# Attention's preparation in a new order: loads ahead of operand copies, norms of six heads on GpSimd, decoding by slot 94

## The chip, the cores and the metric

The program runs on one core of one Trainium2 chip. The metric is device time in microseconds, one launch from start to end. The core's engines are TensorE (PE; its weight loads are listed as PEld), VectorE (DVE), ScalarE (ACT), GpSimd (POOL) and SyncE (SP), which here only issues DMAs. Each engine takes its instructions in the order of the program and stands at one whose semaphores have not come; an instruction that runs on another engine is waited for by semaphore.

## The reference, cut to what matters

```python
# q, k, v: (2, 8, 768, 64); centroids: (8, 16, 64)
q_assign = argmax(einsum('bhsd,hcd->bhsc', q / norm(q), c / norm(c)))     # nearest of 16 centroids
k_assign = argmax(einsum('bhsd,hcd->bhsc', k / norm(k), c / norm(c)))
mask     = q_assign[..., :, None] == k_assign[..., None, :]
scores   = where(mask, q @ k.T / 8, -1e9);  attn = softmax(scores)        # with the maximum taken out
x        = attn @ v                                                       # to (1536, 512)
h = x @ w_in;  x = (max(h, 0) + alpha * min(h, 0)) @ w_out                # 512 -> 2048 -> 512
xn = x / sqrt(mean(x * x) + 1e-6) * rms_g
g = xn @ w_gate;  out = (g * sigmoid(g) * (xn @ w_val)) @ w_out2          # 512 -> 1536 -> 512
```

Everything is float32. The kernel's matmuls run on rounded operands (fp32r) split into a high and a low part.

## The kernel before

Attention takes the 16 heads as 8 pairs. A pair has two phases, one for each half of its queries, and a phase has six slots, one for each tile of 128 keys; so a pair is 12 slots, attention is slots 0 to 95, and slots before 0 prepare. The body of slot s is `st_tile` (L522): for each of the two heads two matmuls make scores (L532, L533) and ScalarE takes the exponential (L534) out of one of three score banks. Every second slot `pv_tiles` multiplies two tiles by the values (L548) and sums them (L553). Nine slots ahead, `max_tile` makes the scores of a later phase once more, without their low parts (L490), into its one bank (two PSUM banks wide), and VectorE takes the maxima (L494); `max_split` and `max_rows` (L499 to L519) put them as two rows into the operand op2. At a phase's end come the sums, their reciprocals and the product (L560 to L598).

A pair is prepared some 40 slots ahead. SP loads the rows ("nat") and their transposes ("raw") of q and k (`load`, L340, L342). ScalarE squares nat (L350); VectorE, or for pair 1 GpSimd in halvings (L361), sums the squares (L364); fourteen small steps on VectorE, on 24 numbers a partition, make the norms (`rnorm`, L321 to L328). ScalarE casts raw to the high part in a stage (L449), GpSimd subtracts for the low part (L454). TensorE makes the similarities with the centroids (L380, L390), VectorE scales them (L397), finds the nearest centroid and writes a one-hot code (L406 to L419), TensorE transposes it (L428). There are two stages, pair by pair in turn, and one nat and one raw tile. SP then copies stage and code into the operands op1 and op2 (`prep_dma_a` L458, `prep_dma_oh` L471, `prep_dma_b` L465 to L467), which have room for two pairs: the copies of pair p stand in slots 12p - 12 to 12p - 10, behind the last score matmul of pair p - 2, and the stage they read is written again by the cast of pair p + 2.

The order of everything is written out by hand. The tables FIRST to PAIR give for each kind of step its slot (relative to the pair's first) and a number that sorts it within the slot; the maxima's slots of phases 0, 2 and 3 stand in AHEAD, the others are LEAD = 9 slots ahead of their use. `plan` puts all of it into slots, and `slot` emits it, so this order is the order of each engine's queue, SP's too:

```python
"load": ((-38, 6.1), (-38, 6.2), (-35, 6.1), (-35, 6.2)),     # PAIR: nat q, nat k, raw q, raw k
"hi": ((-33, 4), (-32, 4)),
at(b - 12, 2.5, self.prep_dma_a, h + e)
at(b - 11 + e, 2.5, self.prep_dma_b, h + e)
```

Behind attention stand two feed-forward layers of TensorE work (`mm3`, L796). Their weights come as 64-bit numbers and are decoded in halves: `decode_step` is one of four steps of a half, two groups on VectorE (L772 to L778), a cast on ScalarE (L785), and the low part on GpSimd or VectorE (L782, L783). The first eight halves, 32 steps, are placed by hand among attention's slots in EARLY and TAIL; TAIL also holds the first up and down projections of the first layer (L842 to L898).

Of the kernel before, what the change touches and what calls it, by code (L numbers as in the profile page):

```python
# [13 lines left out]
ALU = mybir.AluOpType  # L14
# [8 lines left out]
    "load": ((-38, 6.1), (-38, 6.2), (-35, 6.1), (-35, 6.2)),  # L23
# [5 lines left out]
    "sims": ((-30, 1.7), (-29, 1.7)),  # L29
    "scale": ((-29, 5.9),),  # L30
# [9 lines left out]
    "norm": tuple((-27 + n // 5, 5 + (n % 5) / 10) for n in range(14)),  # L40
# [3 lines left out]
    "scale": ((-24, 5.1),),  # L44
    "arg": ((-22, 5), (-21, 5), (-20, 5), (-19, 5), (-17, 5)),
    "oht": ((-13, 1.7),),
}
THIRD = {
    **PAIR,
    "load": ((-27, -0.2), (-27, 6), (-26, 6), (-26, 6.1)),  # L50
    "sq": ((-25, 4), (-24, 4)),
    "ss": ((-24, 5), (-23, 5)),
    "norm": tuple((-23 + n // 5, 5.1 + (n % 5) / 10) for n in range(14)),
# [54 lines left out]
    (-1, 8.5, "decode_step"),
    (-2, 9, "decode_step"),
    (-2, 0.95, "decode_step"),  # L110
    (0, 1.45, "decode_step"),
    (2, 1.5, "decode_step"),
    (1, 10, "decode_step"),
# [18 lines left out]
    (1, 4, "decode_step"),  # L132
    (1, 4.1, "decode_step"),
    (1, 4.2, "decode_step"),
    (1, 4.3, "decode_step"),
    (2, 0.2, "decode_step"),
    (2, 0.3, "decode_step"),
# [38 lines left out]
class Attention:  # L176
# [175 lines left out]
    def prep_ss(self, pr, i):  # L352
# [4 lines left out]
        if pr == 1:  # L357
# [7 lines left out]
        if i == 1:  # L365
            self.norm[pr] = self.rnorm(self.ss.pop(pr), [128, X, 2, 4], f"n{pr % 2}")
# [233 lines left out]
    def plan(self):  # L600
# [3 lines left out]
        def at(s, o, fn, *a):  # L604
            ev.setdefault(s, []).append((o, len(ev.get(s, [])), fn, a))
# [530 lines left out]
```

## Time and profile before

| | |
|---|---|
| median of 3 runs | 943.79 us (941.26 to 945.05) |
| profiled execution | 944.59 us, its span 942.8 us |
| busy of the span | TensorE 878.1, VectorE 609.1, GpSimd 376.9, ScalarE 325.3 us |
| mean granted clock of TensorE | 0.96 |

The profile is one execution, and its times count from the span's start. A row of the timeline gives start and length in us, engine, line, operation, result and operands, and in brackets how long the engine had been idle and what ended that. Matmuls that follow each other overlap. An idle engine costs time only where something that sets the end waits for it.

### The profile page before, as it was taken

The page shows a single profiled execution, that of the slowest core. Times are in us where ns is not written, and L with a number is a line of the kernel's source. Part 1 is how long each engine was busy: PE and PEld are TensorE (multiplying, and loading weights), DVE is VectorE, ACT ScalarE, POOL GpSimd, SP SyncE. Part 2 cuts the span into 40 slices and gives each one's busy share as a digit, 9 for nine tenths or more (in the row PEclk, how much of TensorE's full clock was granted, in tenths as well). Part 3 has the DMA queues.
Part 4 walks back from the last instruction along what each step waited for, and adds up shares of the span by engine and source line. Part 5 has one row for each costly group of instructions (what it writes and reads, how often), then busy time and mean ns, then how long its engine had stood idle before and what let it go on. Part 6 is the DMA issues. An engine that isn't in the chain of part 4 may idle for free.

```text
span 942.8 us, 11565 instructions
## 1 busy us (share of the span) xinstructions
PE 878.1 (93%) x4358; PEld 646.2 (69%) x4358; DVE 609.1 (65%) x928; ACT 325.3 (35%) x623; POOL 376.9 (40%) x301
## 2 busy tenths in 40 slices
PE   6787797887999998999999998999999999999998
PEld 4444454555565656877888777787788888888886
DVE  7865663635546646587877988778995838484222
ACT  4344343345444542334343334443322212221111
POOL 5301102011000035466666767523684637464111
PEclk8599797989999999999999999999999999999999
DMA  6946152707147011121221322100231212120002
GB/s 187 227 125 153 54 121 73 162 32 181 41 108 191 25 61 52 39 73 68 68 67 48 109 79 78 45 1 23 90 104 52 90 45 90 44 68 1 1 24 110
DMA packets 24279, 75.69 MB, mean 80 GB/s; under 512 B 3680, under 2 KB 4896, under 8 KB 24224
## 3 DMA queue, kind: packets, MB, share of 16 engines
q1 hardware_dynamic: 24224, 74.96, 27.7%
q8 instruction: 34, 0.56, 0.2%
q14 instruction: 21, 0.17, 0.1%
HBM read 51.46 MB, written 3.15 MB: 58 GB/s over the span
## 4 chain that ended last, share of the span: by engine, by line
PE 70%; DVE 16%; issue 5%; ACT 4%; DMA 3%; POOL 2%; SPq 0%; ACTq 0%; POOLq 0%; DVEq 0%
PE ps_st L796 23%; PE ps_mx L796 10%; PE ps_pv L796 9%; PE ps_pv L548 7%; PE ps_pr L796 4%; PE ps_mx L490 4%; PE ps_pv L553 4%; PE ps_st L532 3%; DVE dec_a L774 3%; PE ps_st L533 3%; DVE x L898 2%; DVE dec_a L772 2%; DMA nat<-in_qn_dram 1%; DVE mx L494 1%; PE ps_pr L581 1%
## 5 line engine op out<-in xcount | busy, mean ns | idle before, releaser
L494 DVE TENSOR_REDUCE mx<-ps_mx 128x1 f32<-128x768 f32 x93 | 88.9, 956 | 113.0 <-PE ps_mx L490 113.0
L856 POOL TENSOR_TENSOR gl<-v,gh 128x512 fp32r<-128x512 f32 x68 | 94.7, 1393 | 101.0 <-ACT gh L855 101.0
L534 ACT ACTIVATE p<-ps_st 128x384 f32<-128x384 f32 x192 | 83.8, 494 | 63.9 <-PE ps_st L533 62.9
L532 PE MATMUL ps_st<-op 128*128 128x384 f32 x192 | 73.7, 384 | 18.5 <-ACT p L534 18.5
L598 POOL TENSOR_TENSOR x1l<-X,x1h 128x384 fp32r<-128x384 f32 x15 | 15.2, 1015 | 184.0 <-ACT x1h L595 184.0
L796 PE MATMUL ps_st<-x1h,stage 128*128 128x512 f32 x272 | 84.3, 391 | 0.0
L774 DVE SCALAR_TENSOR_TENSOR dec_a<-raw,dec_a 128x512 uint32<-128x512 uint32 x66 | 82.4, 1248 | 2.3
L855 ACT CAST gh<-v 128x512 fp32r<-128x512 f32 x68 | 42.2, 621 | 114.5 <-DVE v L852 64.1
L548 PE MATMUL ps_pv<-p,vnat 128*64 128x384 f32 x384 | 78.1, 531 | 0.0
L852 DVE TENSOR_TENSOR v<-ps_st,t 128x512 f32<-128x512 f32 x36 | 24.8, 690 | 77.1 <-PE ps_st L796 76.9
L848 DVE SCALAR_TENSOR_TENSOR v<-v,alpha,t 128x512 f32<-128x512 f32 x45 | 44.9, 999 | 43.4 <-ACT v L847 43.4
L533 PE MATMUL ps_st<-op 82*128 82x384 f32 x192 | 68.0, 354 | 0.0
L454 POOL TENSOR_TENSOR stage<-raw,stage 128x768 fp32r<-128x768 f32 x16 | 29.0, 1825 | 93.4 <-ACT stage L449 77.8
L490 PE MATMUL ps_mx<-op 80*128 80x384 f32 x186 | 56.4, 386 | 8.8 <-DVE mx L494 8.8
L782 POOL TENSOR_TENSOR dec_a<-dec_a,woh 128x512 f32<-128x512 f32 x27 | 42.9, 1590 | 43.1 <-ACT woh L785 39.6
L490 PEld LDWEIGHTS ps_mx<-op 80*128 80x128 f32 x186 | 33.1, 203 | 38.3 <-issue 18.5
L796 PEld LDWEIGHTS ps_st<-x1h,stage 128*128 128x128 f32 x272 | 50.9, 188 | 10.9
L796 PE MATMUL ps_st<-x1h,wvh 128*128 128x512 f32 x144 | 57.0, 396 | 0.9 <-ACT t L851 0.9
L898 DVE TENSOR_TENSOR x<-ps_mx,x 128x1024 f32<-128x1024 f32 x36 | 43.8, 1218 | 21.6 <-PE ps_mx L796 21.6
L532 PEld LDWEIGHTS ps_st<-op 128*128 128x128 f32 x192 | 38.3, 199 | 27.7 <-ACT p L534 25.4
L796 PE MATMUL ps_st<-x1h,wvl 128*128 128x512 f32 x144 | 56.9, 395 | 0.0
L796 PE MATMUL ps_st<-x1l,wvh 128*128 128x512 f32 x144 | 56.8, 394 | 0.0
(247 smaller groups left out, 2105.1 us busy)
## 6 DMA issues: line engine op xcount, KB each, us to landing
raw<-in_moe_w_out_dram SPq DMA_DIRECT2D x28, 512.0 KB, 3.6
op<-stage SPq DMA_DIRECT2D x32, 384.0 KB, 5.5
raw<-in_moe_w_in_dram SPq DMA_DIRECT2D x15, 512.0 KB, 3.6
raw<-in_moe_w_val_dram SPq DMA_DIRECT2D x12, 512.0 KB, 3.4
raw<-in_moe_w_gate_dram SPq DMA_DIRECT2D x12, 512.0 KB, 3.4
op<-stage SPq DMA_DIRECT2D x16, 288.0 KB, 6.5
nat<-in_qn_dram SPq DMA_DIRECT2D x8, 384.0 KB, 4.3
nat<-in_kn_dram SPq DMA_DIRECT2D x8, 384.0 KB, 5.3
```

The lines of the kernel that those rows point to most:

```text
L490: nc.tensor.matmul(ps[:, g, :self.HS], lhsT=o1[0:80, 0, t * 128:(t + 1) * 128], rhs=o1[0:80, 1, sl], start=True, stop=True)
L494: nc.vector.tensor_reduce(out=self.mx[ph][:, k:k + 1], in_=ps[:, :, :self.HS], op=ALU.max, axis=AX.XY)
L532: nc.tensor.matmul(ps, lhsT=o1[:, 1, ks], rhs=o1[:, 0, qs], start=True, stop=False)
L533: nc.tensor.matmul(ps, lhsT=o2[:, 1, ks], rhs=o2[:, 0, qs], start=False, stop=True)
L534: nc.scalar.activation(out=p[:, e], in_=ps, func=AF.Exp, scale=self.scale)
L548: nc.tensor.matmul(ps[64 * e:64 * e + 64], lhsT=self.vnat[ph // 2][:, e, t0 + y], rhs=P[y][:, e], start=t0 + y == 0, stop=t0 + y == T - 1)
L774: v.scalar_tensor_tensor(out=a, in0=top, scalar=0xC0000000, in1=a, op0=ALU.bitwise_and, op1=ALU.bitwise_or)
L782: eng.tensor_tensor(out=af, in0=af, in1=f(hi), op=ALU.subtract)
L796: self.nc.tensor.matmul(ps, lhsT=a, rhs=b, start=first and i == 0, stop=last and i == len(terms) - 1)
L848: nc.vector.scalar_tensor_tensor(out=v, in0=v, scalar=self.nalpha[:, a], in1=t, op0=ALU.mult, op1=ALU.add)
L856: nc.gpsimd.tensor_tensor(out=lo, in0=v, in1=f(hi), op=ALU.subtract)
L898: nc.vector.tensor_tensor(out=dst, in0=ps, in1=dst, op=ALU.add)
```

## The change

It moves steps between slots and engines; what is computed stays.

- Loads: nat and raw of pairs 5 to 7 go from slots -38 and -35 (relative to the pair) to -41, -39 and -38; pair 4 gets a table of its own, FIFTH, with its raw loads first in slot 13 and its casts three slots later; pair 2's nat loads go from slot -3 to -6, pair 3's stay.
- Norms: for pairs 1, 2 and 3 (six heads) the sums of squares are halvings on GpSimd, and of each Newton round four steps run on GpSimd instead of three on VectorE. The first two and the last three steps stay on VectorE. Pair 1's are put ahead of its second low part.
- Maxima: phase 1's six go from slots -3 to 2 to slots -1 to 4; those of phases 2 and 3 begin one slot later.
- Order within a slot: the scaling right behind the similarities' transposes, the sums' matmul behind the maximum and the score matmuls instead of ahead of them, the similarities behind the product with the values.
- Decoding: all 24 steps of TAIL by slot 94 (-2 from attention's end); ten of them stood in slots 95 to 98. For it the second weight buffer of the down projection is opened with the first pool instead of at attention's end.

```diff
 PAIR = {
-    "load": ((-38, 6.1), (-38, 6.2), (-35, 6.1), (-35, 6.2)),
+    "load": ((-41, 6.1), (-41, 6.2), (-39, 6.1), (-38, 6.1)),
-    "sims": ((-30, 1.7), (-29, 1.7)),
-    "scale": ((-29, 5.9),),
+    "sims": ((-30, 2.5), (-29, 1.7)),
+    "scale": ((-29, 1.75),),
 FOURTH = {
-    "norm": tuple((-27 + n // 5, 5 + (n % 5) / 10) for n in range(14)),
+    "norm": tuple((-27 + n // 6, 5 + (n % 6) / 10) for n in range(17)),
-    "scale": ((-24, 5.1),),
+    "scale": ((-24, 1.75),),
+FIFTH = {
+    **PAIR,
+    "load": ((-37, 6.1), (-37, 6.2), (-35, 1.8), (-35, 1.9)),
+    "hi": ((-30, 4), (-29, 4)),
+    "lo": ((-29, 4.5), (-28, 4.5)),
+}
 THIRD = {
-    "load": ((-27, -0.2), (-27, 6), (-26, 6), (-26, 6.1)),
+    "load": ((-30, 13), (-30, 13.1), (-26, 6), (-26, 6.1)),
-    "norm": tuple((-23 + n // 5, 5.1 + (n % 5) / 10) for n in range(14)),
+    "norm": tuple((-23 + n // 5, 5.1 + (n % 5) / 10) for n in range(17)),
 SECOND = {
-    "norm": tuple((-17 + n // 5, 0.3 + (n % 5) / 100) for n in range(14)),
-    "scale": ((-14, 5),),
-    "arg": ((-13, 5.1), (-12, 5), (-11, 5.1), (-10, 5), (-9, 5.1)),
-    "oht": ((-8, 0.7),),
+    "norm": tuple((-18, 9 + n / 100) for n in range(14)) + tuple((-12, 5 + n / 100) for n in range(3)),
+    "scale": ((-12, 5.1),),
+    "arg": ((-11, 5.1), (-10, 5), (-10, 5.1), (-9, 5), (-9, 5.1)),
+    "oht": ((-8, 2.6),),
 AHEAD = {
     0: (-12, -11, -10, -9, -8, -7),
-    2: (6, 6, 7, 8, 9, 10),
-    3: (10, 11, 12, 13, 14, 15),
+    1: (-1, 0, 1, 2, 3, 4),
+    2: (7, 7, 8, 9, 9, 10),
+    3: (11, 12, 12, 13, 14, 15),
 }
+ASIDE = (1, 2, 3)
 TAIL = (
     (-15, 1.45, "decode_step"),
+    (-14, 9, "decode_step"),
+    (-13, 0.5, "decode_step"),
...
+    (-2, 0.5, "decode_step"),
     (-2, 9, "decode_step"),
-    (-1, 8.5, "decode_step"),
...
-    (1, 4, "decode_step"),
...
-    (2, 0.3, "decode_step"),
+    def rnorm(self, ss, shape, tag, aside=False):
+        g = self.nc.gpsimd
         def newton():
+            if aside:
+                return [
+                    lambda: g.tensor_tensor(out=a, in0=y, in1=ss, op=ALU.mult),
+                    lambda: g.tensor_tensor(out=a, in0=a, in1=y, op=ALU.mult),
+                    lambda: g.tensor_scalar(out=a, in0=a, scalar1=-0.5, scalar2=1.5, op0=ALU.mult, op1=ALU.add),
+                    lambda: g.tensor_tensor(out=y, in0=y, in1=a, op=ALU.mult),
+                ]
     def prep_ss(self, pr, i):
-        if pr == 1:
+        if pr in ASIDE:
-            self.norm[pr] = self.rnorm(self.ss.pop(pr), [128, X, 2, 4], f"n{pr % 2}")
+            self.norm[pr] = self.rnorm(self.ss.pop(pr), [128, X, 2, 4], f"n{pr % 2}", pr in ASIDE)
     def plan(self):
-            tab = (FIRST, SECOND, THIRD, FOURTH, PAIR)[min(pr, 4)]
+            tab = (FIRST, SECOND, THIRD, FOURTH, FIFTH, PAIR)[min(pr, 5)]
-            at(b + (7 if last else 8), -0.5 if last else 0.6, self.out_sums, ph)
-            at(b + (7 if last else 8), -0.4 if last else 0.65, self.out_recip, ph)
+            at(b + (7 if last else 8), -0.5 if last else 1.7, self.out_sums, ph)
+            at(b + (7 if last else 8), -0.4 if last else 1.75, self.out_recip, ph)
     def open(self, early):
-        self.wbuf["wo"] = [self.wpair(one, "wo", 0)]
+        self.wbuf["wo"] = [self.wpair(one, "wo", i) for i in range(2)]
     def more(self, ctx):
-        self.wbuf["wo"].append(self.wpair(one, "wo", 1))
```

## Rows read from the trace of the kernel before

**Rows 1.** Stretches: length, busy us of PE, PEld, DVE, ACT, POOL; clock, DMA share.

```profile
26.40:46.80 20.40, 15.44 (x51) 10.54 (x53) 17.50 (x36) 8.94 (x16) 5.82 (x4) 0.50 0.95 234
...
46.90:81.27 34.37, 27.74 (x180) 14.72 (x176) 21.38 (x59) 13.47 (x29) 3.15 (x2) 0.95 0.35 103
81.27:127.40 46.13, 38.31 (x237) 22.62 (x233) 25.40 (x53) 18.87 (x40) 7.39 (x5) 0.89 0.38 94
127.40:170.37 42.97, 36.54 (x227) 21.39 (x226) 20.76 (x48) 18.46 (x42) 5.84 (x5) 0.88 0.43 106
170.37:212.28 41.91, 35.79 (x225) 21.31 (x225) 21.00 (x48) 18.28 (x41) 5.62 (x4) 0.92 0.45 109
212.28:253.61 41.33, 35.40 (x225) 21.15 (x225) 20.98 (x48) 18.28 (x41) 5.62 (x4) 0.92 0.44 103
253.61:285.82 32.21, 31.31 (x214) 19.35 (x214) 16.46 (x31) 14.89 (x36) 2.01 (x2) 1.00 0.47 109
...
366.00:380.00 14.00, 9.95 (x37) 7.72 (x36) 7.80 (x8) 1.91 (x4) 4.54 (x3) 0.88 0.11 39
```

**Rows 2.** Waits of PE, slots 24 to 59: total us, times, longest.

```profile
PE ps_st L532 <- ACT p L534: 16.3, 9, 4.8
```

**Rows 3.** Timeline of slots 27 to 29.

```profile
146.66 0.83 ACT L449 CAST stage<-raw 128x768 fp32r<-128x768 f32 x1 [7.94 <-DMA vnat<-in_vn_dram]
...
147.93 0.69 PE L532 MATMUL ps_st<-op 128*128 128x384 f32 x1 [4.80 <-ACT p L534]
```

**Rows 4.** Timeline of SP, slots 26 to 28: DMA issues.

```profile
133.39 1.25 SPq L467 DMA_DIRECT2D op<-stage  x1
...
136.76 0.76 SPq L342 DMA_DIRECT2D raw<-in_kt_dram  x1
...
138.78 0.99 SPq L467 DMA_DIRECT2D op<-stage  x1
```

**Rows 5.** DMA issues at 133.39, 136.76, 138.78, 28.21: KB, us to landing.

```profile
op<-stage SPq DMA_DIRECT2D x1, 96.0 KB, 5.3
...
raw<-in_kt_dram SPq DMA_DIRECT2D x1, 384.0 KB, 6.1
...
op<-stage SPq DMA_DIRECT2D x1, 96.0 KB, 7.6
...
op<-stage SPq DMA_DIRECT2D x1, 96.0 KB, 5.2
```

**Rows 6.** Timeline of PE, slots 4 to 6.

```profile
53.16 0.85 PE L380 MATMUL ps_pr<-raw,cb 128*32 128x384 f32 x8
...
56.98 0.49 PE L390 MATMUL ps_pr<-idf,simc 128*128 128x128 f32 x3
...
59.58 0.62 PE L490 MATMUL ps_mx<-op 80*128 80x384 f32 x2 [1.05 <-DVE mx L494]
```

**Rows 7.** Timeline of GpSimd and VectorE, slot 2.

```profile
44.65 3.60 POOL L454 TENSOR_TENSOR stage<-raw,stage 128x768 fp32r<-128x768 f32 x2 [11.25 <-ACT stage L449]
...
44.83 1.69 DVE L315 TENSOR_TENSOR n_a<-n_y,ss 128x24 f32<-128x24 f32 x1
```

**Rows 8.** Instructions of line 315: ns, least, median, most.

```profile
L315 DVE TENSOR_TENSOR n_a<-n_y,ss x24: 173/182/1696, 8.1 to 229.4; 128x24 f32<-128x24 f32 x24
```

**Rows 9.** Timeline of slots -9 to 0.

```profile
28.21 1.53 SPq L467 DMA_DIRECT2D op<-stage  x1
...
34.85 1.01 PE L490 MATMUL ps_mx<-op 80*128 80x384 f32 x2 [2.51 <-DVE mx L494]
...
37.71 0.53 PE L532 MATMUL ps_st<-op 128*128 128x384 f32 x1
```

**Rows 10.** Groups of GpSimd by form: count, busy us, mean ns, idle before.

```profile
L361 POOL TENSOR_TENSOR nat<-nat 128x24 f32<-128x24 f32 x2 | 0.5, 252 | 0.2
```

**Rows 11.** Waits of PE, slots 12 to 23.

```profile
PE ps_pr L581 <- ACT op L519: 2.4, 1, 2.4
```

**Rows 12.** Timeline of PE, the second down projection.

```profile
370.40 0.47 PE L796 MATMUL ps_mx<-gh,woh 128*128 128x512 f32 x1 [4.05 <-DVE x L896]
```

More of the change, by code (lines that the diff above doesn't have):

```diff
@@ L96 @@
     (-15, 1.45, "decode_step"),
+    (-14, 9, "decode_step"),
+    (-13, 0.5, "decode_step"),
+    (-13, 9, "decode_step"),
     (-12, 9, "decode_step"),
-    (-11, 0.5, "decode_step"),
+    (-11, 9, "decode_step"),
+    (-10, 0.5, "decode_step"),
     (-10, 9, "decode_step"),
-    (-8, -0.5, "decode_step"),
-    (-10, 8.95, "decode_step"),
-    (-7, 9, "decode_step"),
-    (-4, 9.0, "decode_step"),
-    (-5, 9, "decode_step"),
+    (-9, 9, "decode_step"),
+    (-9, 9.1, "decode_step"),
+    (-8, 0.5, "decode_step"),
+    (-8, 9, "decode_step"),
+    (-8, 9.1, "decode_step"),
+    (-7, 9, "decode_step"),
+    (-6, 0.5, "decode_step"),
+    (-6, 9, "decode_step"),
+    (-6, 9.1, "decode_step"),
+    (-5, 7, "decode_step"),
+    (-4, 0.5, "decode_step"),
     (-4, 9, "decode_step"),
+    (-4, 9.1, "decode_step"),
     (-3, 9, "decode_step"),
+    (-2, 0.5, "decode_step"),
     (-2, 9, "decode_step"),
-    (-1, 8.5, "decode_step"),
[L109 to L113, printed above, removed]
     (-9, 2.55, "up_part", 0, 0),
@@ L131 @@
     (2, 5, "down_add", 0, 0, 1),
-    (1, 4, "decode_step"),
[L133 to L136, printed above, removed]
-    (2, 0.3, "decode_step"),
     (3, 1, "down_mm", 1, 0, 0),
@@ L305, in warm @@
             self.nc.tensor.matmul(ps, lhsT=self.idr, rhs=self.zero, start=True, stop=True)
-    def rnorm(self, ss, shape, tag):
+    def rnorm(self, ss, shape, tag, aside=False):
         v = self.nc.vector
```

## The prediction

> **What bounds the kernel now.** I read the stages first, in the table of stretches, which I cut where the score matmuls (L532, two in a slot) of slots 0, 12, 24 and so on begin [rows 1]. Slots 60 to 71 compute a pair of heads with nothing of a later pair prepared beside it: 32.21 us, TensorE busy 31.31, granted clock 1.00 (2.4 GHz). The five pairs before it compute the same and take 46.13, 42.97, 41.91, 41.33, and, in slots 0 to 11 (37.7 to 81.27), 43.57. That is 216 us against five times 32.2, 161. The two feed-forward layers behind attention keep their code. So attention's first 60 slots and its last few are what can move.
>
> Then the waits, to see what ends TensorE's idle time there. In slots 24 to 59 nearly all of it is a score matmul that waits for the exponential of an earlier tile [rows 2]: the score banks are full because ScalarE is late. The timeline says why: in slot 27 ScalarE stands for 7.94 us in front of the cast at L449, until 146.66, and TensorE loses 4.80 [rows 3]. The same wait is there one and two pairs later.
>
> What does the cast wait for? It reads a raw tile and writes a stage. The second raw load was issued at 136.76 and took 6.1, so it was there at 142.9, before the cast. But the stage still had readers, the operand copies of two pairs ago: the last was issued at 138.78, took 7.6, and landed at 146.4 [rows 4, 5]. That is the moment at which the cast goes on. So it waits for the copies, and the raw loads matter because they stand in front of those copies: the group of copies ahead of them landed at 133.39 + 5.3 = 138.7, they at 142.9. They hold the queue for 4.2 us.
>
> **The three pairs of slots 24 to 59.** For pairs 5, 6 and 7 the change puts the raw loads (and the nat loads) ahead of that group of copies, into slots 19 to 22, 31 to 34 and 43 to 46, where the last reader of their tile, in slot 20, 30 or 42, has run. The casts stay in slots 27 and 28, the copies in 24 to 26. The copies then land up to 4.2 us earlier, and TensorE's 4.80 becomes 0.6; the other bound is half of the 4.2 (if the copies' own many small pieces set the pace), which leaves 2.7. I take 0.6, as both groups follow the other traffic directly. A pair then costs 32.21, plus the matmuls that prepare a later pair: 0.85 and 0.49 for the similarities [rows 6], some 0.4 for three lighter transposes, 1.75 together. The low clock behind each long wait (stretch clocks 0.88, 0.92, 0.92) goes with the wait. That is 33.96 + 0.6.
>
> A new cost: the low parts (L454) on GpSimd now run in slot 28, where VectorE has its norm steps; till now most of those came before them. How that looks is seen at 44.65: two subtractions on GpSimd take 3.60, and beside them a VectorE step on 24 elements takes 1.69 [rows 7], where the middle one of its kind takes 0.18 [rows 8]. The maximum behind such steps comes late, and TensorE needs its bank. Bounds: 0, and 3.4 for two such steps; I take 1.0, since VectorE is busy for only 21 us of such a pair and catches up. Pair: 35.6; three: 106.8 instead of 126.2. Gain 19.4, bounds 24.3 (neither wait) and 3 (2.7 of wait, 3.4 of VectorE, and 1.0 to 1.7 of low clock in each).
>
> **Start, up to slot 12.** TensorE now reaches slot 0 behind three maxima of phase 1, and these come behind fourteen norm steps on VectorE: the second maximum waits 2.51 for VectorE, and slot 0 begins at 37.71 [rows 9]. The change leaves one maximum in front of slot 0 and puts twelve norm steps of pair 1 on GpSimd. Slot 0 can then begin when the last copies for head 1 are there, 28.21 + 5.2 = 33.4 [rows 9, 5]: four us earlier. It doesn't run fast at once: from 26.4 to 46.8 the granted clock is 0.50 (1.2 GHz) with TensorE busy 76%, and the DMA engines are at 95% [rows 1]. ScalarE's squares and casts of pair 2 stand between the first exponentials and wait for loads on those engines, so I let slot 3 begin near 43.5 instead of 50. Slots 3 to 11 run 1 us shorter: VectorE is freed there of 24 norm steps at 0.18 to 1.7 each and of four sums of squares, but TensorE waits 1.05 in each slot with two maxima, as at 59.58, because they share one bank [rows 6]; two such slots stand there now (6, 10) and two then (7, 9). Gain 7.5, bounds 4 and 10.
>
> GpSimd's price: the trace has no norm step on it. The nearest row is the addition with 24 results, 0.252 us [rows 10]; twelve with small gaps are 3.6 a pair. The squares of pairs 2 and 3 that go with them are six halvings for q and for k, from 384 wide down to 12; between 0.252 for 24 and 1.8 for 768 wide they make about 3 each, an estimate from these rows. That is 10 us a pair on an engine that is busy for 7.39 of the 46 us of slots 12 to 23 [rows 1]. Bounds for a step: 0.2 and 1.8.
>
> The Trainium skill (GPSIMD Engine Reference, 4.1 Engine selection) speaks against this move: elementwise work on two inputs belongs on VectorE, GpSimd being about twice as slow. The rows give 0.252 against 0.18, so 1.4 times at this width. By the page's ratio twelve steps would be about 4.9 with the gaps, and the sum 1.3 higher if pair 1's norms set the start; by the rows they end before the loads for which ScalarE waits.
>
> **Middle, slots 12 to 23.** The casts of pair 4 go from slots 15 and 16 to 18 and 19, when the copies out of their stage have long landed. So the 2.4 that TensorE stood in slot 16 behind ScalarE [rows 11] is gone, and the low clock behind it. The sums' matmul goes behind the maximum, and the scaling goes first on VectorE, so that one waits less for the other. At clock 1.00 the work of a pair is 31.3, plus 2.2 of preparation (three of its four parts and one twice), plus one more maximum and one more row of maxima, 1.3: 34.8. I leave 4.1 idle: 2.1 in two slots with double maxima, the usual 0.9 (32.21 - 31.31), 1.1 of small waits. 38.9 instead of 46.13: gain 7.2, bounds 4 (the clock falls as now) and 9.4.
>
> In slot 13 SP takes pair 4's raw loads ahead of two groups of copies and waits there for a low part on GpSimd. Behind it stand copies for slot 24 alone: no cost, and it would take GpSimd ten slots late to make one.
>
> **End.** At 370.40 TensorE has waited 4.05 for its bank [rows 12], which VectorE has not copied out because the last decoding steps stand ahead, and then runs some 3.4 us at the lower clock (0.88 over 14 us), 1.7 more [rows 1]. The change has all 24 steps done by slot 94, so 5.75 is to be had. But ten more steps crowd into slots 81 to 94. TensorE has no idle time there now, and VectorE's steps stretch beside GpSimd as above. I leave 1.0 for it, bounds 0 and 3.8. Gain 4.8.
>
> **Sum.** 7.5 + 7.2 + 19.4 + 4.8 = 38.9. The profiled execution took 944.6, so 905.7; the median of the runs lies 0.8 lower: 905. With every gain at its lower bound it would be 931, with every one at its upper 894.
>
> **Rivals.**
> 1. *The copies land as late as before*, or VectorE takes it back beside GpSimd. The casts wait on, and the three pairs give 3 to 8: 919. For it: the cast waits for copies that don't move in the order. Against: the 4.2 between two landings.
> 2. *GpSimd holds VectorE in slots 0 to 23.* Each of its two-input steps waits for the GpSimd instruction under way; ten steps at 1.69 for 0.18 give back the 14.7 of start and middle: 919.5. Against: most of GpSimd's new pieces are 0.25 long, and a step waits no longer than a piece. The Trainium skill (GPSIMD Engine Reference, 1. Specifications) names this contention, for two SBUF inputs and for VectorE's two-port modes; the rows agree for the first.
> 3. *Slower*: a norm step on GpSimd costs as much as its 768-wide subtraction, 1.8. Then twelve are 21.6, and the maxima of pairs 1, 2 and 3 wait for them: 3 times 18 is 54, more than the 38.9 gained, 959. It decides from 1.4 a step; the row of 0.252 speaks against it.
> 4. *The early loads don't start early*, because SP still stands at a wait ahead of them. Then the end and a little of the start remain: 938. Against it: the waits of SP in these slots are those of the copies themselves, and the loads now come first.
>
> **How the numbers follow.** Forecast 0.66 (its own range 896 to 914), rival 1 0.17, rival 2 0.09, rival 3 0.03, rival 4 0.05. The range, 892 to 923, takes in the upper bounds, rivals 1 and 2, and 2 us for the spread of the runs. 0.5%, 4.7 us, is about what a measurement of this kernel can't tell from no change. Faster by more: the forecast, both 919s and half of rival 4, 0.94; within it 0.03; slower 0.03.
>
> **What would show it.** In slots 27 to 53 ScalarE waits 3 to 4 us at L449 instead of 7.4 to 7.9, TensorE under 1, and a pair takes 35 to 36. The first score matmul comes at 33 to 34, slot 12 near 74, slot 24 near 113. GpSimd's norm steps take 0.2 to 0.3. No wait is left at the second down projection. I am wrong if the copies land no earlier, if reductions on VectorE lag behind L454, or if the clock stays at 0.50 long past slot 3.

## The result and the profile after

The kernel after takes 908.53 us (median of 4 runs, 905.67 to 912.34) against 942.52 for the kernel before beside it (4 runs, 940.48 to 945.05): ratio 0.9641, 95% interval 0.9593 to 0.9688. That is 34 us less, where 905 was predicted. The profiled execution of after took 905.67, span 903.9.

In the kernel after the lines stand some 17 further down: the casts are L466, the low parts L471, the maxima L507 and L511, the scores L549 to L551, the sums' matmul L584, the norm steps on GpSimd L326 to L329. The table of stretches of after, cut like [rows 1] (columns as there; the first row is a window of the start, then slot 0 to 3, 3 to 12, 12 to 24, two of the three pairs, slots 60 to 71, and the second down projection):

```profile
26.40:46.80 20.40, 16.84 (x71) 10.34 (x72) 14.88 (x24) 10.13 (x19) 15.14 (x32) 0.67 0.99 228
33.21:45.42 12.21, 9.62 (x40) 5.66 (x40) 9.38 (x15) 5.93 (x11) 10.36 (x22) 0.69 1.03 246
45.42:74.43 29.01, 24.60 (x169) 14.27 (x168) 19.13 (x41) 13.99 (x30) 15.28 (x36) 1.00 0.49 137
74.43:113.39 38.96, 34.76 (x239) 21.15 (x235) 26.88 (x55) 18.33 (x40) 7.40 (x5) 1.00 0.50 132
113.39:148.63 35.24, 33.05 (x227) 20.07 (x226) 23.57 (x48) 18.17 (x42) 5.85 (x5) 1.00 0.53 130
148.63:183.79 35.16, 33.18 (x225) 19.97 (x225) 23.57 (x48) 17.99 (x41) 5.64 (x4) 1.00 0.53 130
...
219.02:251.96 32.94, 31.69 (x215) 19.53 (x214) 16.36 (x31) 14.80 (x36) 2.00 (x2) 1.00 0.46 107
...
357.00:371.00 14.00, 14.00 (x62) 11.41 (x61) 11.25 (x14) 5.44 (x10) 7.52 (x6) 1.00 0.17 53
```

By the starts of the score matmuls the spans differ so:

| stage | before | after | gain | forecast |
|---|---|---|---|---|
| to slot 12 | 81.27 | 74.43 | 6.8 | 7.5 |
| slots 12 to 23 | 46.13 | 38.96 | 7.2 | 7.2 |
| slots 24 to 59 | 126.21 | 105.63 | 20.6 | 19.4 |
| slots 60 to 83 | 64.35 | 65.81 | -1.5 | 0 |
| from slot 84 on | 624.84 | 619.07 | 5.8 | 4.8 |
| sum | | | 38.9 | 38.9 |

The sum of the profiled executions is the forecast's, and that is luck in part: the stages miss it by -0.7, 0, +1.2, -1.5 and +1.0, which cancel. That execution of after was also the lowest of its four runs; the gain between the medians is 34.

The waits of TensorE in slots 24 to 59 of after, to set beside [rows 2]: eighteen, none longer than 0.7.

```profile
PE ps_st L549 <- ACT p L551: 6.2, 18, 0.7
```

The timeline of after at the cast of pair 5, to set beside [rows 3]:

```profile
128.88 0.84 ACT L466 CAST stage<-raw 128x768 fp32r<-128x768 f32 x1 [3.82 <-DMA vnat<-in_vn_dram]
...
130.15 0.44 PE L549 MATMUL ps_st<-op 128*128 128x384 f32 x1 [0.66 <-ACT p L551]
```

SP's issues of after (the last raw load of this pair and the last copies out of its stage) and then what two of them took to land, in the order 106.53, 122.77, to set beside [rows 4, 5]:

```profile
106.53 0.44 SPq L359 DMA_DIRECT2D raw<-in_kt_dram  x1
...
122.77 1.43 SPq L484 DMA_DIRECT2D op<-stage  x1
```

```profile
raw<-in_kt_dram SPq DMA_DIRECT2D x1, 384.0 KB, 3.8
...
op<-stage SPq DMA_DIRECT2D x1, 96.0 KB, 5.9
```

The raw tile was there at 110.3, 18 us before the cast. The cast went on at 128.88, and the copies landed at 122.77 + 5.9 = 128.7. So what it waits for is the copies, though the profile names another transfer of that queue. It is so everywhere: in all fourteen profiles of this document, the first cast of each of the three pairs begins 0.22 to 0.31 after the last copy out of its stage has landed. Counted from the start of slot 24, they are issued at 9.4 instead of 11.4 and land at 15.3 instead of 19.0: 3.7 earlier.

GpSimd's norm steps, by form, between 20 and 113 us (count, busy us, mean ns of one, idle before), and then the two engines at the first low part of pair 5, to set beside [rows 7, 10]:

```profile
L329 POOL TENSOR_TENSOR n_y<-n_y,n_a 128x24 f32<-128x24 f32 x9 | 2.4, 272 | 0.7
L328 POOL TENSOR_SCALAR n_a<-n_a 128x24 f32<-128x24 f32 x9 | 2.4, 262 | 0.7
L327 POOL TENSOR_TENSOR n_a<-n_a,n_y 128x24 f32<-128x24 f32 x9 | 2.3, 255 | 0.7
L326 POOL TENSOR_TENSOR n_a<-n_y,ss 128x24 f32<-128x24 f32 x9 | 2.2, 243 | 5.0 <-DVE n_y L340 4.6
```

```profile
129.79 3.62 POOL L471 TENSOR_TENSOR stage<-raw,stage 128x768 fp32r<-128x768 f32 x2 [10.46 <-ACT stage L466]
...
130.05 1.62 DVE L332 TENSOR_TENSOR n_a<-n_y,ss 128x24 f32<-128x24 f32 x1
131.70 1.75 DVE L333 SCALAR_TENSOR_TENSOR n_a<-n_a,n_y 128x24 f32<-128x24 f32 x1
```

What nobody had forecast stands in slots 60 to 71: 32.94 instead of 32.21, with nothing prepared beside them. The timeline of TensorE in slot 62 of after shows the sums' matmul in its new place, behind a wait of the score matmuls for ScalarE:

```profile
224.46 0.44 PE L549 MATMUL ps_st<-op 128*128 128x384 f32 x1 [0.19 <-ACT p L551]
...
225.28 0.73 PE L584 MATMUL ps_pr<-sel,ssb 128*128 128x2 f32 x6
```

In its old place, between two slots' score matmuls, it filled the time in which ScalarE caught up. Now four groups of score matmuls follow one another, TensorE waits, and the sums come on top: 0.73 for a pair of two phases.

### The profile page after: what moved, and what is told of

Read it like the earlier page. It is cut to its first block, busy times and chain, and to the rows that moved or that the text cites. A ratio compares the mean times of both kernels' runs of the same rounds, so it can differ in the third digit from the quotient of the medians.

```text
span 903.9 us, 11594 instructions
## 1 busy us (share of the span) xinstructions
PE 860.2 (95%) x4358; PEld 636.6 (70%) x4358; DVE 610.9 (68%) x897; ACT 323.9 (36%) x623; POOL 395.8 (44%) x361
## 4 chain that ended last, share of the span: by engine, by line
PE 69%; DVE 14%; ACT 6%; issue 4%; POOL 3%; DMA 2%; SPq 2%; ACTq 0%; POOLq 0%; DVEq 0%
PE ps_st L812 24%; PE ps_mx L812 10%; PE ps_pv L812 10%; PE ps_pv L565 6%; PE ps_pr L812 5%; PE ps_pv L570 3%; PE ps_mx L507 3%; DVE dec_a L790 3%; PE ps_st L549 3%; DVE x L914 2%; PE ps_st L550 2%; DVE dec_a L788 2%; DMA op<-stage 2%; ACT p L551 1%; DVE mx L511 1%
## 5 line engine op out<-in xcount | busy, mean ns | idle before, releaser
L511 DVE TENSOR_REDUCE mx<-ps_mx 128x1 f32<-128x768 f32 x93 | 88.9, 956 | 86.5 <-PE ps_mx L507 86.5
L872 POOL TENSOR_TENSOR gl<-v,gh 128x512 fp32r<-128x512 f32 x68 | 94.6, 1391 | 105.6 <-ACT gh L871 104.1
L551 ACT ACTIVATE p<-ps_st 128x384 f32<-128x384 f32 x192 | 83.1, 496 | 50.5 <-PE ps_st L550 50.1
L549 PE MATMUL ps_st<-op 128*128 128x384 f32 x192 | 71.7, 374 | 11.8 <-ACT p L551 11.8
L864 DVE SCALAR_TENSOR_TENSOR v<-v,alpha,t 128x512 f32<-128x512 f32 x45 | 43.9, 974 | 43.9 <-ACT v L863 43.9
L565 PE MATMUL ps_pv<-p,vnat 128*64 128x384 f32 x384 | 73.2, 502 | 0.0
L550 PE MATMUL ps_st<-op 82*128 82x384 f32 x192 | 65.5, 341 | 0.0
L507 PE MATMUL ps_mx<-op 80*128 80x384 f32 x186 | 54.1, 372 | 6.1 <-DVE mx L511 6.1
L914 DVE TENSOR_TENSOR x<-ps_pv,x 128x1024 f32<-128x1024 f32 x35 | 42.6, 1218 | 20.5 <-PE ps_pv L812 20.5
L507 PEld LDWEIGHTS ps_mx<-op 80*128 80x128 f32 x186 | 31.5, 193 | 34.6 <-issue 11.9
L549 PEld LDWEIGHTS ps_st<-op 128*128 128x128 f32 x192 | 36.6, 190 | 25.7 <-ACT p L551 24.1
```

The costliest lines, as they stand in the source:

```text
L507: nc.tensor.matmul(ps[:, g, :self.HS], lhsT=o1[0:80, 0, t * 128:(t + 1) * 128], rhs=o1[0:80, 1, sl], start=True, stop=True)
L511: nc.vector.tensor_reduce(out=self.mx[ph][:, k:k + 1], in_=ps[:, :, :self.HS], op=ALU.max, axis=AX.XY)
L549: nc.tensor.matmul(ps, lhsT=o1[:, 1, ks], rhs=o1[:, 0, qs], start=True, stop=False)
L550: nc.tensor.matmul(ps, lhsT=o2[:, 1, ks], rhs=o2[:, 0, qs], start=False, stop=True)
L551: nc.scalar.activation(out=p[:, e], in_=ps, func=AF.Exp, scale=self.scale)
L565: nc.tensor.matmul(ps[64 * e:64 * e + 64], lhsT=self.vnat[ph // 2][:, e, t0 + y], rhs=P[y][:, e], start=t0 + y == 0, stop=t0 + y == T - 1)
```

## The experiments

Twelve kernels ran, in three groups (runs 1 to 4, 5 to 8, 9 to 12), each beside the kernel before on the same chip (medians 943.75, 941.73 and 944.24 there). The stages are lengths in us in the one execution that was profiled, from the starts of the score matmuls; "slot 12" is when it starts. In runs 2, 4 and 7 that execution was the longest of its runs (925.38, 921.16 and 917.58).

| kernel | median us (runs) | ratio, 95% | slot 12 | 12-23 | 24-59 | 60-83 | from 84 |
|---|---|---|---|---|---|---|---|
| after | 908.53 (4) | 0.9641, 0.9593 to 0.9688 | 74.4 | 39.0 | 105.6 | 65.8 | 619.1 |
| 1 before, early loads only | 928.87 (4) | 0.9848, 0.9825 to 0.9872 | 80.9 | 46.8 | 109.5 | 64.4 | 625.6 |
| 2 loads back | 923.50 (4) | 0.9792, 0.9768 to 0.9816 | 78.3 | 39.0 | 121.5 | 65.8 | 619.0 |
| 3 copies a slot later | 911.05 (4) | 0.9663, 0.9634 to 0.9692 | 76.8 | 39.0 | 109.6 | 65.8 | 619.0 |
| 4 sums in front | 913.89 (6) | 0.9699, 0.9664 to 0.9735 | 77.0 | 41.9 | 116.5 | 64.3 | 619.7 |
| 5 norms on VectorE | 918.67 (4) | 0.9737, 0.9687 to 0.9788 | 80.7 | 43.9 | 105.9 | 65.8 | 619.0 |
| 6 decoding back | 916.46 (4) | 0.9731, 0.9687 to 0.9775 | 75.6 | 42.0 | 105.4 | 65.8 | 625.4 |
| 7 maxima back | 916.03 (4) | 0.9722, 0.9705 to 0.9739 | 82.2 | 38.9 | 109.9 | 65.8 | 619.0 |
| 8 sums split | 907.75 (4) | 0.9635, 0.9619 to 0.9652 | 74.0 | 38.9 | 108.7 | 64.4 | 619.8 |
| 9 second maxima behind | 912.92 (5) | 0.9662, 0.9637 to 0.9688 | 73.3 | 45.8 | 107.4 | 65.8 | 619.1 |
| 10 casts apart | 904.85 (5) | 0.9585, 0.9562 to 0.9608 | 76.5 | 39.0 | 103.4 | 65.8 | 619.0 |
| 11 all three (8, 9, 10) | 907.40 (5) | 0.9608, 0.9583 to 0.9633 | 74.0 | 45.7 | 101.3 | 64.3 | 619.7 |
| 12 after again | 908.57 (6) | 0.9615, 0.9589 to 0.9642 | 74.0 | 39.0 | 105.4 | 65.8 | 619.0 |

**1. The early loads alone.** The kernel before with one more table:

```diff
+EARLIER = {**PAIR, "load": ((-41, 6.1), (-41, 6.2), (-39, 6.1), (-38, 6.1))}
-            tab = (FIRST, SECOND, THIRD, FOURTH, PAIR)[min(pr, 4)]
+            tab = (FIRST, SECOND, THIRD, FOURTH, PAIR, EARLIER)[min(pr, 5)]
```

> The kernel before, with the raw and nat loads of pairs 5 to 7 alone moved ahead of the copies. Theory (the casts wait for the operand copies of two pairs ago, and those stand behind the raw loads in the queue): the casts in slots 27, 39 and 51 wait 3.5 to 4 us instead of 7.4 to 7.9, TensorE loses under 1 us in each, slots 24 to 59 take about 106 to 109 us instead of 126.2, and the whole is 17 to 20 us faster, ratio 0.979 to 0.982. Rival 1 (the copies land as late as before): 3 to 8 us, ratio 0.992 to 0.997, and the casts still wait 7 us. All stages but slots 24 to 59 stay as before by both.

The three pairs of this run, in the table of stretches:

```profile
127.73:163.35 35.62, 33.08 (x227) 19.83 (x226) 23.71 (x48) 18.34 (x42) 5.85 (x5) 1.00 0.53 128
163.35:201.48 38.13, 34.42 (x225) 20.73 (x225) 20.99 (x48) 18.18 (x41) 5.62 (x4) 0.96 0.49 120
201.48:237.20 35.72, 33.22 (x225) 19.73 (x225) 23.88 (x48) 18.14 (x41) 5.63 (x4) 1.00 0.43 98
```

They take 109.5 instead of 126.2, so 16.7 come from the loads alone; by the medians it is 0.0152 of 942, 14.3. Rival 1 gave them 3 to 8 and is out. It is some 3 us under the theory, and one pair shows why: in the first and third the cast waits 3.8 and TensorE 0.6 to 0.7, as expected, but in the second the last copy took 6.9 us to land instead of 5.6 or 5.7, the cast waited 5.22, TensorE 2.07, and 3.4 us at a granted clock of 0.50 followed.

**2. The loads back.** The kernel after with PAIR's old loads:

```diff
-    "load": ((-41, 6.1), (-41, 6.2), (-39, 6.1), (-38, 6.1)),
+    "load": ((-38, 6.1), (-38, 6.2), (-35, 6.1), (-35, 6.2)),
```

> The kernel after, with the loads of pairs 5 to 7 back at their old slots. Theory: the three pairs go back to 41 to 43 us each from 35.2, 17 to 21 us, and the wait of the casts to over 7 us; the whole is 923 to 928, ratio about 0.983. If the 20.6 us in slots 24 to 59 come instead from the matmuls that moved inside a slot (similarities, scaling, sums), which this run keeps, the pairs stay under 38 us, and the time under 915.

Slots 24 to 59 take 121.5, 15.9 more than in after; the medians differ by 15.0. The timeline shows the old wait at the cast, and behind it TensorE's:

```profile
136.22 0.83 ACT L466 CAST stage<-raw 128x768 fp32r<-128x768 f32 x1 [7.28 <-DMA op<-stage]
...
137.50 0.69 PE L549 MATMUL ps_st<-op 128*128 128x384 f32 x1 [4.13 <-ACT p L551]
```

The casts of the three pairs wait 7.28, 6.19 and 6.52, two of them less than the 7 that was expected. So the loads are worth 15 to 17 of the 20.6, from both sides. The other 4 to 5 could lie in the order inside a slot, which run 1 lacks and run 2 keeps, or in what differs from one execution to the next, as in the second pair of run 1; run 4 looks at the order.

**3. The copies a slot later.**

```diff
-                at(b - 11 + e, 2.5, self.prep_dma_b, h + e)
+                at(b - 10 + e, 2.5, self.prep_dma_b, h + e)
```

> The kernel after, with the second group of operand copies (three per head) issued one slot later, for all pairs from 2 on; no load moves. If the cast waits for these copies (they read the stage that it writes), its wait grows by a slot, about 2.9 us, from 3.8 to 6.5 or more, TensorE loses some 2 to 4 us in each pair, and the whole is 6 to 15 us slower than after, ratio 0.970 to 0.98. If the cast waits for its raw load, its wait stays at 3.8 and the time at that of after, ratio about 0.964.

This one can't tell. SP does nothing else between the groups, so a later slot changed only one place in its queue, a load of values and three copies before slot 24; the copies for the cast of slot 27 were issued from 3.1 to 9.4 after slot 24 in both kernels, and the cast waited 4.06 instead of 3.82. What waits for what was settled above by the landing times. The run serves as a repeat: the four computing engines have the instructions of after in the same order, yet two of its three pairs take 37.1 and 37.7, at a granted clock of 0.95. In these two the last copy took 6.0 and 6.5 us to land (5.9 and 5.6 in after), TensorE waited 0.91 and 1.40 behind the cast (0.66 and 0.43), and 3.4 us at 0.50 followed each.

**4. The sums in front again.**

```diff
-            at(b + (7 if last else 8), -0.5 if last else 1.7, self.out_sums, ph)
-            at(b + (7 if last else 8), -0.4 if last else 1.75, self.out_recip, ph)
+            at(b + (7 if last else 8), -0.5 if last else 0.6, self.out_sums, ph)
+            at(b + (7 if last else 8), -0.4 if last else 0.65, self.out_recip, ph)
```

> The kernel after, with the matmul of the sums and the reciprocal behind it back ahead of the score matmuls of their slot, 0.6 and 0.65 instead of 1.7 and 1.75. Reading of the profile after: slots 60 to 83 take 65.81 instead of 64.35, 0.36 us per phase, since four groups of score matmuls now follow one another and wait 0.19 us for the exponential. By that, slots 60 to 83 go back to 64.4, and all 16 phases give 3 to 5 us: 903 to 905 by the median, ratio about 0.960. Rival: in slots 0 to 59 the sums in front make the maximum late on VectorE, as was meant to be mended, and take back 1 to 5 us there: ratio 0.962 to 0.966, with slots 60 to 83 at 64.4 all the same.

The gain in slots 60 to 83 came, they go back to 64.3; but slots 24 to 59 take 116.5, in the longest of the six executions (921.16), and not for the rival's reason, as TensorE waits for no maximum there. The timeline of TensorE in slots 40 and 44, and then the stretch of that pair:

```profile
174.30 0.44 PE L549 MATMUL ps_st<-op 128*128 128x384 f32 x1 [1.82 <-ACT p L551]
...
185.11 0.80 PE L584 MATMUL ps_pr<-sel,ssb 128*128 128x2 f32 x6 [0.74 <-DVE sims L414]
```

```profile
156.59:198.07 41.48, 37.77 (x225) 21.70 (x225) 20.99 (x48) 18.15 (x41) 5.64 (x4) 0.88 0.44 110
```

The sums use the bank in which the similarities of a later pair stand until VectorE has scaled them. In front, TensorE waits 0.74 for that, once a pair, and the granted clock is 0.88 or 0.95 in all three pairs. Only two of the four stretches at 0.50 begin behind that wait; the other two begin behind waits of 1.31 and 1.82 for the cast, where the copies landed later than in after. Run 1 has the same three waits of 0.74 with no stretch at 0.50 behind any, and its two pairs at clock 1.00 take 35.6 and 35.7 against 35.2 in after. So at equal clock the order is worth 0.4 to 0.5 a pair. The rest of the 4 to 5 us goes with late copies and low clock; that the order causes these isn't shown. By the medians the new place is worth 5.4 in the whole kernel.

**5. The norms on VectorE.**

```diff
-        if pr in ASIDE:
+        if pr == 1:
-            self.norm[pr] = self.rnorm(..., pr in ASIDE)
+            self.norm[pr] = self.rnorm(..., False)
-        self.norm[pr][0][i]()
+        if i < len(self.norm[pr][0]):
+            self.norm[pr][0][i]()
```

> The kernel after, with the norm steps of pairs 1 to 3 and the sums of squares of pairs 2 and 3 back on VectorE, in the places that the change gives them. Theory (VectorE is freed by the move and GpSimd's pieces are short): slot 0 begins 2 to 3 us later, behind fourteen norm steps ahead of the one maximum, slots 0 to 23 take 1 to 4 us more, and the whole is 3 to 6 us slower than after, ratio 0.967 to 0.971. Rival (GpSimd held VectorE, so the move itself cost time): slots 0 to 23 get shorter, and the time is 1 to 5 us below that of after, ratio 0.959 to 0.963. Slots 24 and later are the same by both.

The timeline of TensorE in slot 4 (lines stand one further down here), and the stretches of slots 0 to 11, of slots 12 to 23, and of the first 9 us of these:

```profile
50.13 1.01 PE L508 MATMUL ps_mx<-op 80*128 80x384 f32 x2 [2.66 <-DVE mx L512]
```

```profile
33.59:80.65 47.06, 37.64 (x208) 21.33 (x207) 34.30 (x77) 20.04 (x40) 6.89 (x4) 0.83 0.57 154
80.65:124.53 43.88, 39.75 (x238) 23.02 (x235) 26.74 (x54) 18.39 (x40) 7.38 (x5) 0.86 0.44 115
80.65:90.00 9.35, 8.30 (x32) 4.15 (x29) 2.72 (x5) 2.16 (x5) 0.00 (x0) 0.51 0.33 72
```

Ten us slower by the medians (nine by the ratios), where the theory had 3 to 6; rival 2 had the sign wrong. TensorE waits 6.5 for maxima between slots 0 and 12 instead of 3.5. Slots 12 to 23 have the same waits as in after, 4.1 in all; their 4.9 more are low clock, 0.51 over their first 9 us. It fell at 79.59, before slot 12, behind a wait of 0.66 for VectorE that after lacks and one of 0.92 that after has too. The run moves the steps back to VectorE but leaves them in the places of after, so it doesn't show what the engine alone is worth in the places of before.

**6. The decoding back.** TAIL of before in the kernel after; the second weight buffer stays where the change opens it.

```diff
 TAIL = (
     (-15, 1.45, "decode_step"),
-    (-14, 9, "decode_step"),
...
+    (1, 4, "decode_step"),
...
+    (2, 0.3, "decode_step"),
```

> The kernel after, with the 24 decoding steps at the slots of before. Theory: the wait of about 4 us at the second down projection and the low clock behind it come back; from slot 84 on 624 to 625 us instead of 619.0, and slots before 84 don't change; the whole is 5 to 6 us slower than after, ratio 0.969 to 0.971. Rival (ten steps more in slots 81 to 94 cost there what they save): slots 60 to 83 or 84 to 95 get shorter by 1 to 4 us, and the whole is within 2 us of after.

The wait is back (waits of TensorE, slots 84 to 390 us), from slot 84 on it takes 6.4 more, and nothing before slot 84 gets shorter by the tail: the ten steps are free in slots 81 to 94.

```profile
PE ps_mx L812 <- DVE x L912: 4.2, 1, 4.2
```

The median is 7.9 over that of after. The two profiled executions differ by 10.4: 6.4 from slot 84 on, 3.1 in slots 12 to 23 and 1.1 before them, where this run has the instructions of after. Its stretch of slots 12 to 23, to set beside that of after above:

```profile
75.56:117.59 42.03, 37.82 (x239) 22.96 (x235) 26.95 (x55) 18.44 (x40) 7.40 (x5) 0.92 0.48 122
```

TensorE's five waits there are those of after, 1.05, 1.05, 0.62, 0.95 and 0.45, in the same places. The 3.1 more are low clock alone.

**7. The maxima back.**

```diff
-    1: (-1, 0, 1, 2, 3, 4),
-    2: (7, 7, 8, 9, 9, 10),
-    3: (11, 12, 12, 13, 14, 15),
+    2: (6, 6, 7, 8, 9, 10),
+    3: (10, 11, 12, 13, 14, 15),
```

> The kernel after, with the maxima of phases 1 to 3 at the slots of before: three of phase 1 ahead of slot 0 instead of one, phases 2 and 3 a slot earlier. Theory: slot 0 begins at 35 to 37 instead of 32 to 33.2, and the time to slot 12 grows by 2 to 4 us, since the score matmuls could have run while the third maximum waits; ratio 0.966 to 0.969. Rival: the same matmuls are done on either side of slot 0, and slots 0 to 11 get shorter by what slot 0 is later; slot 12 stays at 74.4 to 78.3 and the time at that of after.

Slot 0 begins at 36.5, as in the theory, but slot 12 at 82.2, 4 to 8 later than in after and in runs 2, 3, 6, 8, 10 and 12. Slots 24 to 59, where TensorE has the instructions of after, take 4.3 more: TensorE's waits there are 1.1 longer in all, 0.93 and 1.38 instead of 0.66 and 0.43 behind two casts whose copies landed late, and both times 3.4 us at 0.50 follow. One of the new waits before slot 12, on TensorE before slot 1 (lines one further up here):

```profile
41.09 0.58 PE L533 MATMUL ps_pr<-idr,mh 128*64 128x128 f32 x3 [2.28 <-DVE sims L413]
```

**8. The sums in front where nothing stands in their bank.**

```diff
-            at(b + (7 if last else 8), -0.5 if last else 1.7, self.out_sums, ph)
+            at(b + (7 if last else 8), -0.5 if last else 0.6 if ph >= 10 or ph in (3, 5, 7, 9) else 1.7, self.out_sums, ph)
```

(and the reciprocal 0.05 behind.)

> The kernel after, with the sums' matmul ahead of the score matmuls in those phases alone where no scaled similarity stands in its bank: phases 3, 5, 7 and 9 and all from 10 on; phases 0, 1, 2, 4, 6 and 8 keep the new place. Reading of the run with all of them in front: in front costs TensorE 0.74 in the phases that follow the similarities, and the clock falls behind such waits, while it gives 0.36 in each of the other phases. By that, each of the nine phases gives 0.36, 3 us in all: slots 24 to 59 about 104.5 instead of 105.6 and slots 60 to 83 64.35 instead of 65.8; 905 to 906 by the median, ratio about 0.961. Rival: the clock falls more often in slots 24 to 59 than in after, and takes 3 us or more back: ratio 0.964 or above.

```profile
112.94:147.94 35.00, 32.83 (x228) 19.98 (x226) 23.76 (x48) 18.18 (x42) 5.87 (x5) 1.00 0.53 130
147.94:184.85 36.91, 34.58 (x225) 20.44 (x225) 23.91 (x48) 17.98 (x41) 5.63 (x4) 0.95 0.51 123
```

The small gain is there (64.35 in slots 60 to 83), and two things take it back. From slot 84 on it takes 0.7 more, as do the two other kernels with these sums in front (runs 4 and 11). And two of the pairs have the clock at 0.95 in this execution, as the rival has it, though not behind the sums: the stretches at 0.50 begin behind TensorE's waits of 0.96 and 0.77 for the cast. The median is that of after within the measurement.

**9. The second maximum of a slot behind other matmuls.**

```diff
-                at(s, 0.5 if s % 2 or s < 0 else 1.5, self.max_tile, ph, k)
+                o = 0.5 if s % 2 or s < 0 else 1.5
+                again = s > 0 and any(g[2] == self.max_tile for g in ev.get(s, ()))
+                at(s, (1.2 if s % 2 else 2.2) if again else o, self.max_tile, ph, k)
-                at(mid, 1.6, self.max_split, ph, 0)
+                at(mid, 2.3 if slots[1] == mid > 0 and mid % 2 == 0 else 1.6, self.max_split, ph, 0)
```

> The kernel after, with the second maximum of a slot that has two moved behind the score matmuls (odd slots) or behind the matmuls with V (slot 12, and the split that follows it); all else stays. Theory (the 1.05 that TensorE waits there is the first maximum's reduction, in the one bank of the maxima): the waits in slots 6, 8, 12 and 14 shrink from 1.05 to 0.4 or less, 2.5 to 3.5 us in all, and 0 to 3 us more where the low clock behind them goes; slots 0 to 23 that much shorter, ratio about 0.958 to 0.961. Rival: the wait moves to the score matmuls or to the rows of maxima that now come later, and nothing is gained: ratio 0.964.

In slots 6 and 8 the wait shrinks from 1.05 to 0.35. In slots 12 to 15 it moves to the rows of maxima, as the rival has it, and the clock falls to 0.50 in between (timeline of TensorE, then the stretches of slots 12 to 23 and of slot 14):

```profile
81.44 0.58 PE L534 MATMUL ps_pr<-idr,mh 128*64 128x128 f32 x3 [1.34 <-DVE mh L517]
...
93.26 0.39 PE L534 MATMUL ps_pr<-idr,mh 128*64 128x128 f32 x3 [1.32 <-DVE mh L517]
```

```profile
73.29:119.06 45.77, 40.57 (x239) 24.82 (x235) 29.50 (x57) 18.47 (x40) 7.39 (x5) 0.85 0.45 112
81.82:90.06 8.24, 8.24 (x33) 5.00 (x32) 3.04 (x6) 2.80 (x5) 0.00 (x0) 0.50 0.93 230
```

**10. The casts apart**, in slots 28 and 32 of a pair instead of 27 and 28:

```diff
-    "hi": ((-33, 4), (-32, 4)),
-    "lo": ((-32, 4.5), (-31, 4.5)),
+    "hi": ((-32, 4), (-28, 4)),
+    "lo": ((-32, 4.5), (-28, 4.5)),
```

> The kernel after, with the two casts of pairs 5 to 7 in slots 28 and 32 (and 40, 44, and 52, 56) instead of 27 and 28, each in an even slot, and their low parts in the same slots. Theory: by then the operand copies have landed, so ScalarE waits under 1 us at the first cast instead of 3.7, TensorE's idle 0.66 and 0.23 behind it go, 0.4 to 0.9 us a pair: slots 24 to 59 take 103.5 to 105 without low clock instead of 105.6; ratio 0.961 to 0.963. Rival: the low part in slot 32 or the cast there makes a new wait of its own, and the pairs take 35.2 or more.

```profile
115.51:149.64 34.13, 32.83 (x227) 20.07 (x226) 23.75 (x48) 18.23 (x42) 5.89 (x5) 1.00 0.55 134
149.64:184.93 35.29, 32.94 (x225) 19.94 (x225) 22.47 (x48) 18.01 (x41) 5.66 (x4) 1.00 0.54 129
184.93:218.90 33.97, 32.68 (x226) 20.01 (x225) 23.42 (x48) 18.13 (x41) 5.67 (x4) 1.00 0.45 103
```

The pairs take 103.4. ScalarE still waits 3.3, 4.4 and 2.6 at the first cast, so that part of the theory was wrong: it gets there before the copies either way, but now behind two more exponentials, and TensorE loses nothing in the first and third pair (1.07 in the second). The median is 3.7 under that of run 12 on the same chip; the two intervals overlap a little.

**11. Runs 8, 9 and 10 together.**

> The kernel after, with the split places of the sums (3, 5, 7, 9 and from 10 on in front), the second maxima behind, and the casts in slots 28 and 32, together. Theory: the gains add, 3 plus 3 plus 2, and less of the low clock, since less of TensorE's idle time is left: 898 to 903 by the median, ratio 0.953 to 0.958. Rival: what is gained in waits is lost to the granted clock as in the run with the split places alone: 905 to 908, ratio 0.961 or above.

```profile
119.67:153.47 33.80, 32.64 (x227) 19.98 (x226) 23.81 (x48) 18.22 (x42) 5.89 (x5) 1.00 0.54 135
153.47:187.32 33.85, 32.73 (x225) 19.85 (x225) 23.94 (x48) 18.01 (x41) 5.67 (x4) 1.00 0.55 135
187.32:220.94 33.62, 32.50 (x226) 19.86 (x225) 23.92 (x48) 18.03 (x41) 5.67 (x4) 1.00 0.46 104
```

The pairs are the shortest of all, 101.3, and slots 60 to 83 64.3; but slots 12 to 23 bring run 9's low clock along, 45.7, and the median, 907.40, is where the rival had it. With after's 39.0 there its profiled 906.9 would be about 900, an estimate from these stages; the kernel with 8 and 10 alone wasn't tried.

**12. The kernel after again.**

> The kernel after, unchanged, on the chip of the other three, so that they can be told from it and its own spread is seen. If its profiled run, 905.67, was the lowest by luck of the granted clock, the median lies at 907 to 911, ratio 0.962 to 0.967, and slots 0 to 23 differ by 2 to 5 us from one profile to the other with the same instructions; if not, the median is near 905.7 and the stages repeat within 1 us.

The median repeats, 908.57, and the runs go from 904.91 to 911.92. Its profiled execution was again the lowest of its runs, and its stages are those of after within 0.5. The other part of the expectation is seen across runs: up to slot 12 the kernels of runs 2, 3, 6, 8 and 10 have the instructions of after on the computing engines, and reach slot 12 at 78.3, 76.8, 75.6, 74.0 and 76.5 instead of 74.4 and 74.0. TensorE's waits between slots 0 and 12 are not the same in them, 5.2 us in all in run 12 and 8.4 in run 2. Run 2 lost most of it in slot 8, shown here beside slot 8 of after:

```profile
60.42:69.84 9.42, 8.37 (x33) 4.55 (x33) 4.24 (x9) 2.28 (x5) 4.62 (x11) 0.64 0.24 86
```

```profile
59.70:65.96 6.26, 5.21 (x34) 3.05 (x33) 4.46 (x9) 2.27 (x5) 4.58 (x11) 1.00 0.02 4
```

## Why the prediction was right, and where it was not

- **The casts wait for operand copies, and the raw loads hold the queue ahead of those.** Shown, by the landing times (the raw tile 18 us early in after, the copies 0.22 to 0.31 before the cast in every profile) and by runs 1 and 2. ScalarE's waits fell to 3.6 to 3.8, TensorE's to 0.43 to 0.66, as forecast (3 to 4, and 0.6).
- **The size of that step was too large.** It took all 19.4 of the three pairs for the loads. Runs 1 and 2 give them 15 to 17. Of the other 4 to 5, the order of scaling and sums within a slot is 0.4 to 0.5 a pair at equal clock (run 1 against after); the prediction counted it for slots 12 to 23 alone, and left out the 0.74 that TensorE waited for the scaling in each of these pairs of before. The rest is late copies and low clock, and no run ties it to the order.
- **VectorE beside GpSimd, 1.0 a pair, did not come.** The stretched steps are there, 1.62 and 1.75 for 0.18, but TensorE waits no more than 0.23 to 0.25 in the slot that follows. Against it stand 0.73 a pair for the sums behind the maximum, which no step of the prediction had. The two errors nearly cancel, so that 35.2 came out beside the forecast 35.6, by luck; in slots 60 to 83, where only the second is there, it shows as 1.5.
- **Start.** Slot 0 at 33.21 (33.4 forecast, when the copies land). The match is luck: slot 0 doesn't wait for the last copies of head 1, which landed at 33.74 in after. In run 12 it begins at 32.12, and only its fourth score matmul waits for them, 0.47, until 33.75. Slot 3 at 45.42 instead of 43.5, and slots 3 to 11 in 29.0 instead of 31.2, 2.2 shorter and not 1. Sum 6.8 for 7.5. Runs 5 and 7 show that both parts, the norms and the maxima, carry it: each undone alone costs 7 to 10 us by the median, which is more than their theories gave (2 to 6). In the profiles part of it lies in later slots: 4.9 in slots 12 to 23 of run 5, all low clock at the waits of after, and 4.3 in slots 24 to 59 of run 7, of which 1.1 is longer waits for late copies and the rest low clock. By the profiles run 7 loses 3.9 to 8.2 up to slot 12, run 5 2.4 to 6.7.
- **Middle.** 38.96 for 38.9, with five waits of 4.1 in all.
- **End.** 5.8 for 4.8. The 1.0 kept for crowded slots was not needed: run 6 shows that the ten steps cost nothing where they went.
- **Profile to median.** The prediction set the median 0.8 under the profiled execution. For after it is 3 above it, 4 above in run 12. That, and no stage, is the difference between the predicted 905 and 908.5. The two longest of them have more low clock: the mean granted clock over the span of the four of after, 905.67, 906.97, 910.08 and 912.34 us, is 0.989, 0.989, 0.985 and 0.983. In which stages it fell is not known, as those executions have no profile.
- **Rivals.** 1: out by runs 1 and 2. 2: out by run 5, which came out with the opposite sign. 3: a norm step takes 0.24 to 0.27, where 1.4 would have decided. 4: the raw loads of pair 5 were issued 6 us ahead of the first copies behind them, so they started early. The ratio that the Trainium skill gives (GPSIMD Engine Reference, 4.1 Engine selection, about twice as slow) is not reached here: 0.243, 0.255 and 0.272 for the three two-input steps against 0.18 on VectorE, 1.3 to 1.5 times. The move paid although each step got slower, since VectorE was what TensorE waited for (run 5: 6.5 for maxima instead of 3.5).

What stays open is what decides the low clock. In run 6 and after, the same instructions with the same five waits ran once at 0.92 and once at 1.00. In slots 24 to 59 of after and of all runs but run 2, TensorE has 21 waits of 0.74 to 2.07; behind twelve of them a stretch at 0.50 begins within 2.6 us, behind nine none does, and without such a wait none begins. Two things vary there that no run set: the last copy takes 5.4 to 7.3 us to land, which sets TensorE's wait for the cast, and then the clock falls or doesn't.

## What to carry to other kernels

When an engine stands in front of an instruction, compare the landing times of all that it needs: here the tile it reads had been there for long, and the tile it writes was still being read, by copies queued behind a load that nobody needed yet; moving the load was worth 15 us. Before moving a small matmul, ask which bank it shares and what it filled: the sums cost a wait of 0.74 a pair in one place, 0.36 a phase in the other. When stages are compared between two executions, look at the granted clock of each stage first, as a stage of 39 us was 42 with the same instructions and waits, and at the wait that stands ahead of each fall: it may come from a transfer that landed late, and not from the change that is tried.

## What the runs showed of the hardware

- The granted clock is not a function of the instructions: slots 12 to 23 had 1.00 in the runs 2, 3, 8, 10, 12 and after, 38.9 to 39.0 us, and 0.92 in run 6, 42.0 us. Six runs of one kernel spread over 7 us (904.91 to 911.92).
- Waits of one us can cost more through the clock than by themselves: two waits of 1.3 on the rows of maxima (runs 9 and 11) went with 8.2 us at 0.50 in slot 14, which takes 6.49 in after, and the stage grew by 6.8 both times, while TensorE's waits grew by 1.0.
- An issue that SP is free to make happens when SP gets to it: a slot later in the written order moved nothing, the copies of slot 24 were issued from 3.1 to 9.4 us after its start in after and in run 3.
- The same copy of 96 KB, issued 9.1 to 9.8 us after the start of a pair with the loads out of its way, took 5.4 to 7.3 us to land (after and all runs but run 2).
- A step on VectorE with two inputs that starts beside a GpSimd subtraction of 768 numbers a partition lasts until that ends, 1.62 and 1.75 us instead of 0.18.
